# One scheduler, new durations: the order of a gated-scan and two-FFN kernel planned anew

## The chip, the cores and the metric

The kernel runs on one core of one Trainium2 chip, in float32. The metric is the device time of one execution in microseconds (us); lower is better. Shorter durations are given in nanoseconds (ns).

## The reference

Three stages follow each other, for batch 4, 8 heads, 768 steps, head width 48 (so a model width of 384) and a hidden width of 1024.

```python
for t in range(S):                       # 1: gated scan, per head
    state = alpha[t][:, None] * state + outer(k[t], v[t])
    y[t] = q[t] @ state
xk = mu_k*x + (1-mu_k)*x_prev            # 2: first FFN, x_prev is x one step earlier
xr = mu_r*x + (1-mu_r)*x_prev
x  = sigmoid(xr @ w_r) * (relu(xk @ w_k)**2 @ w_v)
h  = relu(x @ w_in)                      # 3: second FFN, 3-tap convolution over time as a gate
out = (h * sigmoid(conv(h, conv_w))) @ w_out
```

## The kernel before

The scan is done by chunks of 128 steps (24 chunks, c = 0 to 23), and the two FFNs by units of 256 steps (12 units, u = 0 to 11; three units make one batch entry). For a chunk, `prep(c)` loads alpha, k, q and v and makes the decays on VectorE: it turns the inputs to lie with the head width on partitions (on TensorE for c < 5, by three 128x512 VectorE transposes after that), runs two VectorE scans over 128x512 elements (`bt`, the suffix products, and `gt`, their counterpart for q), and multiplies k and q with them (`kd`, `qd`). `attend(c)` makes the scores and the state's update, in groups of small matmuls, and `advance(c)` the chunk's output `xt`. In a steady unit the program names, in this order, `stage_k` (x @ w_k and its square, into `bigh` and `bigl`), `stage_r` (the gate), `attend`, `stage_v` (@ w_v, gated, into the pair `xh`, `xl`), `advance` and `prep` two chunks ahead, `stage_h` (@ w_in, the convolution and its gate on VectorE and ScalarE, by eight blocks of 128 hidden columns), the second chunk, the mixes for the next unit, and `stage_o` (@ w_out). Nearly every matmul is made of three: a number is split in a high part and a low part (`xh`, `xl`; `wih`, `wil` and so on), and the product leaves out low times low. Units 0 and 1 are computed while the weights still arrive, with undivided w_r and w_v.

None of this is executed in the order in which it is named. Every call on `pl` (an object of the class `Plan`) only notes an operation with what it depends on and how long it should take. `Plan.cost` gives the duration from the engine, the operation and the elements of a row; `Plan.part` begins a group of matmuls with a fixed extra; `Plan.lag` is the time from one engine's end to another's start, with the transfer time for a DMA. Each operation gets a `tail`, the longest way from its start to the end of the program. `Plan.forward` then plays the program through: on the engine that can begin earliest it takes the operation that is ready, and of several that are ready the one with the longest tail. An operation is not broken off once it has begun. `Plan.backward` computes the tails again from the order found. `Plan.issue` repeats this six times and keeps the order with the earliest modelled end; the instructions are then issued engine by engine in that order, and each engine keeps to it on the chip, waiting where an input is late. Transfers have one queue, SP's, ordered in the same way. Where the plan sees TensorE idle before 30 us, it puts in small matmuls on `ones` ("warm" matmuls), whose results nothing uses.

Which instructions there are is thus the same whatever the durations are, the warm matmuls excepted; their order on each engine, and which buffer each takes, come from the durations. All instructions are recorded at line 303 of the kernel, so that the profile names them by their tiles.

Of the kernel before, what the change touches and what calls it, by code (L numbers as in the profile page):

```python
# [138 lines left out]
class Plan:  # L139
# [58 lines left out]
    def cost(self, eng, fn, args, kw, n):  # L198
        ptr = sum(is_ap(x) and self.size(x) == 1 for x in (*args[1:], *kw.values()))
        ptr = ptr if n > 1 else 0  # L200
        if eng == "vector":
            tensors = sum(is_ap(x) and self.size(x) > 1 for x in (*args[1:], *kw.values()))
            fast = fn in ("tensor_copy", "tensor_scalar") and tensors == 1 and "accum_out" not in kw
            fast = fast and not self.in_psum(args[1])
            return 70 + (0.52 if fast else 1.04) * n + 62 * ptr
        if eng == "scalar":
            return 93 + 0.833 * n + 93 * ptr
        if eng == "gpsimd":
            return 60 + 0.8 * n if fn == "memset" else 150 + (2.1 if fn == "tensor_tensor" else 1.0) * n
        if eng == "sync":  # L210
            return 475.0
        if fn == "transpose":
            return 109.0
        x = args[1].on(args[1].pool.tiles[0]) if isinstance(args[1], Buf) else args[1]
        if x.dtype == F32R:
            return n / 2.2

        rows = 64 if x.shape[0] <= 64 else 128
        width = next(w for w in (32, 64, 128) if self.size(args[1]) <= w)
        return 4 * n / 2.4 * rows / 128 * width / 128 + 3  # L220
# [13 lines left out]
    def part(self):  # L234

        if self.whole:
            self.ops.append(self.whole)
        self.whole = self.op("tensor")
        self.whole.dur += 200.0

    def op(self, eng):
        op = Op()
# [83 lines left out]

    def lag(self, op, s):
        t = self.LAG[op.eng][list(self.LAG).index(s.eng)]
        return t + 650 + op.bytes / 360 if op.bytes else t

    def forward(self, start, spare, until):
        order, free, clock = [], dict.fromkeys(self.LAG, start), Clock()
        dma, flying = start, [0.0] * 8
        todo = {e: [] for e in free}
        for op in self.ops:
            op.left, op.ready = len(op.deps), 0.0
            for r in op.root:
                r.left, r.end, r.tile, r.line.n, r.line.held = len(r.ops), 0.0, None, 0, 0
                r.pool.free = [(0.0, i) for i in range(len(r.pool.tiles))]
            if not op.left:  # L340
                insort(todo[op.eng], (-op.tail, op.i, op))
        for _ in self.ops:
            t, op = self.pick(todo, free)
            e = op.eng
            todo[e].remove((-op.tail, op.i, op))
            dur = op.dur
            if e == "tensor":
                x = free[e]
                idle = min((f for f in spare.free if f[0] < x), default=None) if x < until else None
                while idle and x + 115 * clock.at(x) < t - 50:  # L350
                    x += clock.spend(x, 113.0, 1.0) + 2
                    order.append(spare.tiles[idle[1]])
                    spare.free = [(x + 200, i) if i == idle[1] else (f, i) for f, i in spare.free]
                dur = clock.spend(t, dur, op.share)
            for r in op.root:
                if r.tile is None:
                    r.line.n += 1
                    r.line.held += 1
                    f = min(r.pool.free)
                    r.pool.free.remove(f)  # L360
                    r.slot, r.tile = f[1], r.pool.tiles[f[1]]
            free[e] = op.end = t + dur
            if op.bytes:
                dma = op.end = max(dma, op.end + 650) + op.bytes / 360
                flying = flying[1:] + [dma + 900]
                free[e] = max(free[e], flying[0])
            for s in op.succ:
                s.left -= 1
                s.ready = max(s.ready, op.end + self.LAG[e][list(self.LAG).index(s.eng)])
                if not s.left:  # L370
                    insort(todo[s.eng], (-s.tail, s.i, s))
            for r in op.root:
                r.left -= 1
                r.end = max(r.end, op.end + 150)
                if not r.left:
                    r.line.held -= 1
                    r.pool.free.append((r.end, r.slot))
            order.append(op)
        return order
# [56 lines left out]
def is_ap(x):  # L436
    return isinstance(x, (Buf, bass.AP))
# [704 lines left out]
```

## Time and profile before

| | us |
|---|---|
| time, median of 3 runs | 586.3 (585.58 to 587.22) |
| time of the profiled execution | 584.05 |
| its span, from the first to the last instruction | 582.3 |
| TensorE matmul busy | 559.6 (96%) |
| TensorE weight loads busy | 525.2 (90%) |
| VectorE busy | 492.7 (85%) |
| ScalarE busy | 431.3 (74%) |
| GpSimd busy | 15.8 (3%) |
| mean granted TensorE clock | 0.988 |

The span is what the profiler saw between the first and the last instruction; the execution's own time has 1.75 us around it. In the profile PE is TensorE's matmul stream, PEld its weight loads, DVE is VectorE, ACT is ScalarE, POOL is GpSimd, and SPq the queue that issues transfers. Matmuls are pipelined: one of 256 columns is shown with some 280 ns from start to end, while the next begins much earlier. How fast TensorE really goes is read from the distance between starts.

### The profile page before, as it was taken

What the parts mean: (1) busy time and instruction counts of PE and PEld (TensorE: products, weight loads), DVE (VectorE), ACT (ScalarE), POOL (GpSimd) and SP (SyncE); (2) the same over time, 40 slices, a digit from 0 to 9 for tenths busy, and PEclk for the clock granted to TensorE, in tenths of its full rate; (3) what the DMA queues carried; (4) which work ended last, traced back from release to release, by engine and by line L of the source; (5) the groups of instructions that cost most, each with busy time, mean ns of one, the idle gap of its engine ahead of it and who ended that gap; (6) DMA issues with size and microseconds to landing.
All of it is one profiled execution on the core that took longest, in us unless ns stands there. A gap on an engine that the chain in (4) does not pass through costs nothing.

```text
span 582.3 us, 18585 instructions
## 1 busy us (share of the span) xinstructions
PE 559.6 (96%) x7762; PEld 525.2 (90%) x7762; DVE 492.7 (85%) x1044; ACT 431.3 (74%) x1035; POOL 15.8 (3%) x61
## 2 busy tenths in 40 slices
PE   8679899999989999999999999999999999999997
PEld 7568788999889998998999998998999998999994
DVE  7999999999999889789699789789699789448263
ACT  4799998997668678668668668669659758748563
POOL 3000000000000001000000001000000001000000
PEclk9889999999979999999999999999999999999999
DMA  9998947002432332233132232232132121000000
GB/s 181 213 190 244 247 139 217 16 28 79 113 77 75 73 87 63 56 90 80 40 89 67 54 90 55 66 89 69 51 90 54 41 65 23 22 1 13 18 1 32
DMA packets 87404, 47.99 MB, mean 82 GB/s; under 512 B 49170, under 2 KB 81810, under 8 KB 87314
## 3 DMA queue, kind: packets, MB, share of 16 engines
q1 hardware_dynamic: 87314, 46.74, 32.9%
q8 instruction: 62, 1.02, 0.8%
q14 instruction: 28, 0.23, 0.1%
HBM read 42.00 MB, written 4.72 MB: 80 GB/s over the span
## 4 chain that ended last, share of the span: by engine, by line
PE 60%; DVE 27%; ACT 7%; issue 3%; DMA 1%; POOL 1%; SPq 0%; DVEq 0%; POOLq 0%; ACTq 0%
PE pf L303 52%; DVE tmp L303 7%; PE sc L303 6%; DVE x L303 4%; DVE qd L303 3%; PE kk L303 2%; DVE gt L303 2%; DVE bigl L303 2%; ACT tmp L303 2%; DVE kd L303 2%; ACT raw L303 1%; DVE bt L303 1%; DMA ht<-in_moe_w_v_dram 1%; ACT ht L303 1%; DVE am L303 1%
## 5 line engine op out<-in xcount | busy, mean ns | idle before, releaser
L303 ACT ACTIVATE tmp<-tmp 128x256 f32<-128x256 f32 (+1 forms) x144 | 69.1, 485 | 33.7 <-DVE tt L303 21.6
L303 DVE SCALAR_TENSOR_TENSOR tmp<-ht,cw,tmp 128x256 f32<-128x256 f32 x192 | 86.7, 479 | 5.6 <-ACT tmp L303 4.8
L303 PE MATMUL pf<-bigh,wv 128*128 128x256 f32 x336 | 89.6, 310 | 0.5 <-DVE kd L303 0.3
L303 PE MATMUL pf<-xh,wih 128*128 128x256 f32 x288 | 82.4, 286 | 1.9 <-DVE xl L303 1.0
L303 PE MATMUL pf<-xh,wkh 128*128 128x256 f32 x288 | 79.4, 282 | 3.7 <-ACT xh L303 2.8
L303 PE MATMUL pf<-xl,wih 128*128 128x256 f32 x288 | 81.3, 282 | 1.6 <-DVE xl L303 1.6
L303 PE MATMUL pf<-xl,wkh 128*128 128x256 f32 x288 | 81.3, 284 | 0.6 <-DVE xl L303 0.5
L303 PE MATMUL pf<-xh,wil 128*128 128x256 f32 x288 | 80.9, 281 | 0.0
L303 PE MATMUL pf<-xh,wkl 128*128 128x256 f32 x288 | 80.1, 280 | 0.0
L303 PE MATMUL pf<-bigh,wvh 128*128 128x256 f32 x240 | 68.7, 286 | 1.0 <-DVE bigl L303 0.6
L303 PE MATMUL pf<-bigl,wvh 128*128 128x256 f32 x240 | 67.4, 281 | 0.0
L303 PE MATMUL pf<-woh,bigh 128*128 128x384 f32 x192 | 66.9, 349 | 0.4 <-ACT bigh L303 0.4
L303 PEld LDWEIGHTS pf<-bigh,wv 128*128 128x128 f32 x336 | 63.4, 190 | 3.6 <-ACT x L303 0.6
L303 PE MATMUL pf<-wol,bigh 128*128 128x384 f32 x192 | 65.1, 340 | 0.0
L303 PE MATMUL pf<-woh,bigl 128*128 128x384 f32 x192 | 64.2, 350 | 0.2
L303 ACT ACTIVATE pf<-pf 128x512 f32<-128x512 f32 x88 | 51.1, 584 | 10.9 <-PE pf L303 9.8
L303 PEld LDWEIGHTS pf<-xh,wkh 128*128 128x128 f32 x288 | 54.4, 190 | 4.4 <-ACT xh L303 3.1
L303 PEld LDWEIGHTS pf<-xh,wih 128*128 128x128 f32 x288 | 55.4, 192 | 3.3 <-ACT xh L303 1.3
L303 PEld LDWEIGHTS pf<-xl,wih 128*128 128x128 f32 x288 | 55.3, 192 | 2.1 <-DVE xl L303 2.1
L303 PEld LDWEIGHTS pf<-xl,wkh 128*128 128x128 f32 x288 | 54.8, 190 | 1.6 <-DVE xl L303 1.0
L303 PEld LDWEIGHTS pf<-xh,wil 128*128 128x128 f32 x288 | 55.3, 192 | 0.0
L303 PEld LDWEIGHTS pf<-xh,wkl 128*128 128x128 f32 x288 | 55.0, 191 | 0.0
(164 smaller groups left out, 1391.6 us busy)
## 6 DMA issues: line engine op xcount, KB each, us to landing
vt<-in_v_dram SPq DMA_DIRECT2D x48, 96.0 KB, 3.4
out_dram<-ot SPq DMA_DIRECT2D x23, 192.0 KB, 1.9
sa<-in_alpha_dram SPq DMA_DIRECT2D x38, 96.0 KB, 2.3
sk<-in_k_dram SPq DMA_DIRECT2D x38, 96.0 KB, 2.2
sq<-in_q_dram SPq DMA_DIRECT2D x38, 96.0 KB, 2.3
raw<-in_moe_w_out_dram SPq DMA_DIRECT2D x4, 768.0 KB, 5.3
sk<-in_k_dram SPq DMA_DIRECT2D x38, 80.0 KB, 2.2
sa<-in_alpha_dram SPq DMA_DIRECT2D x38, 80.0 KB, 2.2
```

What stands on the lines that cost most here:

```text
L303: getattr(getattr(self.nc, x.eng), fn)(*args, **kw)
```

## The change

Only the durations of the plan are changed; no operation of the kernel is added, removed or altered.

```diff
@@ def cost(self, eng, fn, args, kw, n):
         ptr = ptr if n > 1 else 0
+        ptr -= kw.get("accum_out") is not None and n > 1
         if eng == "vector":
...
-            return 70 + (0.52 if fast else 1.04) * n + 62 * ptr
+            each = {"tensor_tensor_scan": 2.07, "transpose": 1.7}.get(fn, 0.52 if fast else 1.04)
+            return max(70 + each * n + 62 * ptr, 110)
         if eng == "scalar":
-            return 93 + 0.833 * n + 93 * ptr
+            src = args[1].on(args[1].pool.tiles[0]) if isinstance(args[1], Buf) else args[1]
+            each = 0.81 if self.in_psum(args[1]) else 0.94 if src.ap[-1][0] > 1 else 0.833
+            some = 130 if src.shape[0] == 48 else 0
+            return (65 if each == 0.81 else 93) + each * n + 93 * (ptr + ("accum_out" in kw)) + some
@@ def part(self):
-        self.whole.dur += 200.0
+        self.whole.dur += 250.0
@@ def lag(self, op, s):
-        return t + 650 + op.bytes / 360 if op.bytes else t
+        return t + 650 + op.bytes / 300 if op.bytes else t
@@ def forward(self, start, spare, until):
-                dma = op.end = max(dma, op.end + 650) + op.bytes / 360
+                dma = op.end = max(dma, op.end + 650) + op.bytes / 300
```

In the plan a VectorE scan of 512 elements now takes 1130 ns (602 before), a VectorE transpose of 512 elements 940 ns (602 before), and no VectorE operation less than 110 ns. A ScalarE copy out of PSUM takes 28 ns and 0.023 ns an element less, one that reads every second word 0.107 ns an element more, one on 48 partitions 130 ns more. A group of small matmuls takes 50 ns more, and transfers go at 300 bytes a ns instead of 360.

## Rows read from the trace of the kernel before

**Rows 1.** The page: engine, busy us, share of span, instructions.

```profile
PE 559.6 (96%) x7762; PEld 525.2 (90%) x7762; DVE 492.7 (85%) x1044; ACT 431.3 (74%) x1035; POOL 15.8 (3%) x61
```

**Rows 2.** Windows: stretch, its length, busy us of each engine, clock, DMA share, GB/s.

```profile
core 0: us, PE busy (x) PEld busy (x) DVE busy (x) ACT busy (x) POOL busy (x), PEclk, DMA share, GB/s
0.00:60.00 60.00, 48.84 (x940) 41.73 (x940) 54.03 (x113) 46.67 (x99) 5.95 (x29) 0.94 0.94 207
60.00:105.00 45.00, 41.95 (x413) 37.29 (x414) 44.64 (x79) 41.55 (x87) 0.12 (x1) 1.00 0.66 188
105.00:158.00 53.00, 52.63 (x616) 50.85 (x615) 52.72 (x113) 44.36 (x110) 0.11 (x1) 1.00 0.24 61
159.40:209.30 49.90, 47.03 (x651) 44.76 (x651) 45.87 (x99) 34.03 (x87) 0.11 (x1) 0.93 0.34 82
161.00:169.00 8.00, 6.99 (x33) 6.50 (x34) 7.86 (x15) 3.51 (x10) 0.00 (x0) 0.57 0.53 118
...
209.30:253.80 44.50, 44.30 (x659) 42.05 (x651) 38.41 (x81) 32.11 (x80) 3.17 (x8) 1.00 0.28 68
...
297.40:341.00 43.60, 43.57 (x655) 41.95 (x651) 38.54 (x85) 31.45 (x78) 0.12 (x1) 1.00 0.29 70
```

**Rows 3.** Waits of TensorE from 165 us on: us in total, times, longest.

```profile
PE pf L303 <- DVE bigl L303: 0.6, 1, 0.6
PE pf L303 <- ACT bigh L303: 0.4, 2, 0.2
```

**Rows 4.** TensorE in time: start, us, operation, [idle before <- what ended it].

```profile
157.31 0.28 PE L303 MATMUL pf<-bigh,wvh 128*128 128x256 f32 x1
157.43 0.28 PE L303 MATMUL pf<-bigl,wvh 128*128 128x256 f32 x1
...
159.47 0.38 PE L303 MATMUL pf<-xh,wih 128*128 128x256 f32 x1 [0.38 <-ACT xh L303]
161.00 0.38 PE L303 MATMUL pf<-xl,wih 128*128 128x256 f32 x1 [1.15 <-DVE xl L303]
...
162.42 0.58 PE L303 MATMUL pf<-xh,wih 128*128 128x256 f32 x1 [0.57 <-ACT xh L303]
163.44 0.58 PE L303 MATMUL pf<-xl,wih 128*128 128x256 f32 x1 [0.44 <-DVE xl L303]
163.82 0.42 PE L303 MATMUL pf<-xh,wil 128*128 128x256 f32 x1
164.04 0.42 PE L303 MATMUL pf<-xh,wih 128*128 128x256 f32 x1
```

**Rows 5.** VectorE in time, same columns.

```profile
155.09 1.21 DVE L303 TENSOR_TENSOR_SCAN gt<-ad,rec_f 128x512 f32<-128x512 f32 x1
...
157.07 1.12 DVE L303 STREAM_TRANSPOSE tmp<-sa 128x512 f32<-128x512 f32 x1
158.01 0.77 DVE L303 TENSOR_TENSOR pf<-pf,x 128x512 f32<-128x512 f32 x1
...
159.13 1.23 DVE L303 TENSOR_TENSOR_SCAN bt<-ad,one_l 128x512 f32<-128x512 f32 x1
160.28 0.67 DVE L303 TENSOR_TENSOR xl<-pf,xh 128x512 fp32r<-128x512 f32 x1
...
161.85 1.22 DVE L303 TENSOR_TENSOR_SCAN gt<-ad,rec_f 128x512 f32<-128x512 f32 x1
162.99 0.40 DVE L303 TENSOR_TENSOR xl<-pf,xh 128x256 fp32r<-128x256 f32 x1
```

**Rows 6.** TensorE in time: the next scores after these.

```profile
199.37 0.69 PE L303 MATMUL sc<-qd,kd 48*64 48x64 f32 x32
```

**Rows 7.** Chain that ended last: start, us until the next piece, what.

```profile
46.77 6.15 DMA ht<-in_moe_w_v_dram
...
134.54 1.02 DVE kd L303
...
155.17 1.13 DVE gt L303
```

**Rows 8.** VectorE by form: operation xcount | busy us, mean ns | idle before.

```profile
L303 DVE STREAM_TRANSPOSE kd<-sk 128x512 f32<-128x512 f32 x19 | 21.0, 1106 | 0.0
```

## The prediction

> **What bounds the kernel now.** I read the page first. TensorE's matmuls are busy for 559.6 of 582.3 us, VectorE's instructions for 492.7 [rows 1]. That is a mean over parts with different limits, so I cut the span into windows where the pattern of the page changes [rows 2].
>
> From 0 to 105 us VectorE is the fullest engine: 54.03 of 60 us and then 44.64 of 45. The transfers are busy too, 0.94 of the first 60 us. Here the weights are brought in, narrowed and split, and TensorE fills in. From 105 to 158 us both engines are full: TensorE 52.63 and VectorE 52.72 of 53. From 209 us on TensorE alone is: one unit takes 44.5 or 43.6 us, TensorE is busy for 44.30 or 43.57 of them, and VectorE for about 38.5.
>
> Is a busy TensorE also a fast one? In the list of its instructions in time, matmuls of 256 columns begin 0.12 us apart where nothing disturbs them [rows 4], though each is shown as 0.28 long. From 165 us to the end the view of waits has 1.0 us in all for TensorE [rows 3]. An order alone can therefore win next to nothing behind 165 us.
>
> The one place that stands out lies between. The first `stage_h` matmul of unit 2 begins at 159.47, and to the same point of unit 3 it is 49.90 us, against 43.60 for the unit at the same place of its batch entry, 297.4 to 341.0 [rows 2]. That is 6.3 us too long. The rows of TensorE say why: at the start of `stage_h` it waits 0.38 us for `xh`, 1.15 for `xl`, 0.57 for `xh` and 0.44 for `xl` [rows 4], 2.5 us in all. [...]
>
> What is VectorE doing then? It is never idle there, so this is a question of order. The product `pf<-pf,x` and the two splits `xl` are what TensorE waits for. Ahead of the product stand a `gt` scan and a transpose of alpha, ahead of the first split a `bt` scan, ahead of the second another `gt` scan, each 1.1 to 1.2 us [rows 5]. The transpose and the last two scans belong to `prep(8)`, the ninth of the 24, whose `qd` is first read by the scores at 199.37 [rows 6], some 35 us later. (The chain names a transfer in this stretch, but VectorE's rows run without a gap, so it was not what held the split.)
>
> **The change part by part.** No instruction is removed or added but warm matmuls, so every cost here is that of an order.
>
> The plan's view of VectorE. Per `prep` from chunk 5 on, two scans go from 602 to 1130 ns and three transposes from 602 to 940: 2 x 0.528 + 3 x 0.338 = 2.07 us. Are the new numbers right? In the chain, where a piece lasts until the next instruction can begin, a scan takes 1.13 us and a transpose 1.02 [rows 7]; so the plan was wrong by about that much, and the new one is close. `prep(6)` and `prep(7)` run between 134 and 157 us, in the stretch in which VectorE has no idle time to make good: the old plan has VectorE 2 x 2.07 = 4.1 us earlier there than it is. An order made for that clock sees an idle VectorE and slips in `prep(8)`; on the chip the gap isn't there and the scans delay the product and the splits. With the new durations the same greedy rule finds them ready together at that point and takes the one with the longer tail, which is the product or the split.
>
> [...]
>
> Term A, unit 2. At most the 6.3 us go, at least nothing. I take what the rows price: waits 2.5 us, and the low clock, which follows a stall. At a mean of 0.57, 0.43 / 0.5 x 8 = 6.9 us are at the lower level, of which TensorE works from about 163.8 to 168.5 (an estimate); 4.7 us at half speed lose 2.4. A = 2.5 + 2.4 = **4.9 us**. The work that is put off, the rest of `prep(8)`, must find room: from 209 us on VectorE idles 44.5 - 38.41 = 6.1 us a unit.
>
> Term B, 0 to 105 us. Six preps run here; scans, ScalarE copies and transfers all have other durations, so this order changes as a whole. VectorE is idle for 5.97 + 0.36 = 6.3 us of it [rows 2], some of it before the first data; that bounds the gain. On the other side one more exposed weight transfer costs 6.15 us, as that of `w_v` at 46.77 does [rows 7]. The plan's 300 bytes a ns is still above the 207 GB/s that were moved in the first 60 us, so on the transfers it stays optimistic. I take **0** and keep -6.3 and +6.2.
>
> Term C, from 165 us on. Gain at most the 1.0 us of waits [rows 3]. A loss is possible if preps are put where they hold up `stage_h` (second rival). I take **0**, since TensorE's other work hides VectorE's there now.
>
> The rest: ScalarE's new copy times, some tens of ns each, the 50 ns on a group and the floor of 110 ns change nothing on the chip but through the order, and ScalarE has slack (44.36 of 53 us at its fullest late stretch). Warm matmuls lie in TensorE's idle time at the start, where VectorE and transfers bind; more or fewer cost nothing there. I cost them at 0.
>
> Sum against the profiled execution: 584.05 - 4.9 = 579.2 us. The median of the runs shown is 2.25 us above that execution, so 581.4 us is what I expect of a median.
>
> **The rivals.** First: the stall is traded for another. VectorE is full from 60 to 165 us, so what is not done early must be done later, and the product can be freed only to let the next thing wait, a `kd` for the scores or the mix for unit 3. For it: 52.72 of 53 us. Against it: `prep(8)` has some 35 us to spare. Time: as before, 586.3. [...]
>
> Second, slower: preps planned longer are moved into `stage_h`. In the seven units from 165 to 473 us, VectorE's convolution steps are a chain of their own, and one more transpose (1.02 us) between them that TensorE's other work doesn't cover makes `bigh` late for `stage_o`. Seven times 1.02 are 7.1, less 4.9: 588.5 us; with a scan as well, up to 596. It decides from 4.9 / 7 = 0.7 us a unit. For it: units differ only by where preps stand, and the plan must put 2.07 us more a prep somewhere. Against it: the 1.0 us of waits now, with such instructions already in these places.
>
> Third: the start gets worse by exposed weight transfers, because SP's queue is in a new order too and a load that waits for its buffer holds all behind it. One such transfer leaves 581.4 + 6.15 = 587.5, two give 593.7. For it: transfers are busy 0.94 of the first 60 us; against it: only one of them is in the chain for that long.
>
> **How the numbers follow.** Within 0.3% (1.8 us) is about what a measurement of this kernel can't tell from no change. Forecast, 0.57: its own range is 575 (A whole, and more from the start) to 584.5. First rival, 0.13, and the third with one transfer, 0.06, are within 0.3%. Second rival, 0.18, and the third with two, 0.06, are slower. So faster 0.57, same 0.19, slower 0.24. For the range I leave out two exposed transfers (0.06), the upper part of the second rival (0.07) and a gain of over 11 us (0.06): 575.0 to 590.5 us.
>
> **What would show it.** If A is right, `pf<-pf,x` and `xl` of unit 2 stand ahead of the scans on VectorE, the four waits at the start of its `stage_h` are gone or under 0.5 us each, the clock stays at 1.0 around there, and that unit takes 44 to 45 us instead of 49.9. If B is right, TensorE is full from about 105 us on as before. If C is right, later units stay at 43.6 to 44.5 us. The prediction is wrong if the stretch up to the first full unit moves by more than a few us in either direction: then term B, which I can't price but by bounds, was the larger one. Units of over 45 us would mean the second rival.

## The result, and the profile after

The median went from 586.46 us (585.58 to 587.22, 4 runs) to 570.7 us (570.11 to 571.62, 4 runs): a ratio of 0.9733 [0.9713, 0.9753], 2.7% faster. That is below the range of the prediction. The profiled execution took 570.11 us. Its span is 14.0 us shorter than that of before, and the medians differ by 15.8 us, because the profiled execution of before, which is not one of the four, lay 2.4 us below their median and that of after 0.6 below its own.

The span first, then the engines of the page of after, which answer to [rows 1], and the clock in 40 slices:

```profile
span 568.3 us, 18585 instructions
PE 551.7 (97%) x7778; PEld 522.4 (92%) x7778; DVE 490.8 (86%) x1044; ACT 429.8 (76%) x1035; POOL 15.6 (3%) x61
PEclk9789999999999999999999999999999999999999
```

TensorE's 16 more instructions are warm matmuls (96 instead of 80). The windows of after, cut at the same events as those of [rows 2]:

```profile
core 0: us, PE busy (x) PEld busy (x) DVE busy (x) ACT busy (x) POOL busy (x), PEclk, DMA share, GB/s
0.00:60.00 60.00, 50.89 (x952) 43.70 (x956) 56.52 (x114) 48.50 (x99) 5.98 (x29) 0.91 0.94 209
60.00:105.00 45.00, 43.86 (x498) 39.44 (x488) 43.04 (x82) 40.41 (x89) 0.12 (x1) 1.00 0.62 177
105.00:157.00 52.00, 50.29 (x606) 47.72 (x604) 52.00 (x110) 44.09 (x108) 0.11 (x1) 1.00 0.24 62
157.00:165.00 8.00, 8.00 (x78) 7.97 (x71) 7.46 (x18) 7.01 (x21) 0.00 (x0) 1.00 0.51 117
157.00:200.20 43.20, 43.20 (x660) 41.91 (x652) 42.43 (x93) 31.25 (x81) 0.12 (x1) 1.00 0.35 88
200.20:244.00 43.80, 43.80 (x655) 42.49 (x651) 41.97 (x91) 34.38 (x86) 2.51 (x8) 1.00 0.31 78
286.80:329.90 43.10, 43.10 (x659) 41.82 (x651) 38.65 (x85) 31.25 (x78) 0.33 (x1) 1.00 0.28 72
```

Unit 2 (157.0 to 200.2) takes 43.2 us instead of 49.9, and its first 8 us have a granted clock of 1.00, where 161 to 169 us had 0.57 before. VectorE shows why. In [rows 5] a transpose of `prep(8)` stood ahead of the product, and a scan of `prep(8)` ahead of each of the two splits; after:

```profile
151.96 1.23 DVE L308 TENSOR_TENSOR_SCAN bt<-ad,one_l 128x512 f32<-128x512 f32 x1
153.10 0.67 DVE L308 TENSOR_TENSOR pf<-pf,x 128x512 f32<-128x512 f32 x1
...
154.35 1.22 DVE L308 TENSOR_TENSOR_SCAN gt<-ad,rec_f 128x512 f32<-128x512 f32 x1
155.48 0.66 DVE L308 TENSOR_TENSOR xl<-pf,xh 128x512 fp32r<-128x512 f32 x1
...
157.07 0.41 DVE L308 TENSOR_TENSOR xl<-pf,xh 128x256 fp32r<-128x256 f32 x1
157.40 0.34 DVE L308 TENSOR_TENSOR ss<-ss,tt 128x192 f32<-128x192 f32 x1
157.67 1.08 DVE L308 STREAM_TRANSPOSE tmp<-sa 128x512 f32<-128x512 f32 x1
```

These two scans are the last of `prep(7)`; the first transpose of `prep(8)` now starts at 157.67, behind the last split. TensorE has no wait left at the place of [rows 4]:

```profile
157.03 0.38 PE L308 MATMUL pf<-xh,wih 128*128 128x256 f32 x1
157.25 0.28 PE L308 MATMUL pf<-xl,wih 128*128 128x256 f32 x1
157.36 0.29 PE L308 MATMUL pf<-xh,wil 128*128 128x256 f32 x1
```

For the whole program I cut the span at the first `stage_h` matmul of units 2, 3 and 10, from the list of TensorE's instructions (us). The experiments below are cut at the same events, and each row is one profiled execution:

| kernel | start | unit 2 | units 3 to 9 | rest | span |
|---|---|---|---|---|---|
| before | 159.5 | 49.9 | 308.2 | 64.7 | 582.3 |
| after | 157.0 | 43.2 | 303.4 | 64.7 | 568.3 |
| e1, VectorE's durations | 164.1 | 43.1 | 302.5 | 64.7 | 574.4 |
| e2, all but VectorE's | 161.0 | 49.1 | 308.0 | 64.6 | 582.7 |
| e3, new until unit 2 | 157.6 | 43.6 | 308.5 | 64.7 | 574.4 |
| e4, new from unit 3 | 161.2 | 49.8 | 303.5 | 64.6 | 579.1 |
| e5, `prep(8)` held back | 162.0 | 46.5 | 310.3 | 64.5 | 583.3 |
| e6, short scans, old order | 158.7 | 44.2 | 303.7 | 64.6 | 571.2 |
| e7, VectorE and ScalarE | 162.1 | 43.6 | 303.8 | 64.7 | 574.2 |
| e8, VectorE and transfers | 157.9 | 44.0 | 304.1 | 64.5 | 570.5 |
| e9, scans only | 166.3 | 44.9 | 305.7 | 64.6 | 581.5 |
| e10, transposes only | 157.6 | 45.6 | 304.4 | 65.8 | 573.4 |
| e11, transfers at 330 | 166.9 | 43.1 | 303.5 | 64.6 | 578.1 |
| e12, transfers at 270 | 164.8 | 43.6 | 304.0 | 64.6 | 577.0 |
| e13, 270, no warm matmuls | 162.4 | 43.6 | 303.6 | 64.6 | 574.2 |
| e14, 330, no warm matmuls | 158.5 | 43.1 | 303.5 | 64.7 | 569.8 |
| e15, changed, no warm matmuls | 159.3 | 43.1 | 303.4 | 64.6 | 570.4 |

The 14.0 us are 2.5 of the start, 6.7 of unit 2 and 4.8 of units 3 to 9. Within the start 3.6 us are won up to the first `stage_h` matmul of all (93.1 us instead of 96.7), and 1.1 are lost between there and unit 2: TensorE is busy for 50.29 of 52.00 us from 105 us on, where it was for 52.63 of 53. Units 3 to 9 are the surprise. In the view of waits TensorE's 1.0 us behind 165 us [rows 3] has become 0.5, so it explains 0.5 of the 4.8:

```profile
PE pf L308 <- ACT bigh L308: 0.5, 1, 0.5
```

Where the rest was lost shows in the distance between starts. In units 3 to 9 the time from each matmul on `woh` or `wol` to the next matmul sums to 66.6 us before and to 63.5 after: 3.1 of the 4.8 us are in `stage_o` (0.9 are in the small matmuls, 0.5 in `stage_k`). Unit 4 before, first TensorE, then VectorE:

```profile
272.50 0.34 PE L303 MATMUL pf<-woh,bigh 128*128 128x384 f32 x1
272.68 0.33 PE L303 MATMUL pf<-wol,bigh 128*128 128x384 f32 x1
273.13 0.44 PE L303 MATMUL pf<-woh,bigl 128*128 128x384 f32 x1
273.41 0.33 PE L303 MATMUL pf<-woh,bigh 128*128 128x384 f32 x1
```

```profile
268.93 1.11 DVE L303 STREAM_TRANSPOSE kd<-sk 128x512 f32<-128x512 f32 x1
269.88 1.08 DVE L303 STREAM_TRANSPOSE qd<-sq 128x512 f32<-128x512 f32 x1
270.82 0.40 DVE L303 TENSOR_TENSOR tmp<-tmp,ht 128x256 f32<-128x256 f32 x1
...
272.63 0.44 DVE L303 TENSOR_TENSOR bigl<-tmp,bigh 128x256 fp32r<-128x256 f32 x1
```

Undisturbed, these matmuls start 0.17 to 0.18 us apart. The one on `bigl` starts 0.45 us after its forerunner and 0.06 after the split of `bigl` ends (272.63 + 0.44), with two transposes of a `prep` ahead of that split in VectorE's row, which has no idle time from there to the split. About 0.28 us are lost, and yet no wait is printed and the rows overlap or nearly touch, because a matmul is shown as 0.33 long. The same stage of unit 4 after:

```profile
262.37 0.34 PE L308 MATMUL pf<-woh,bigh 128*128 128x384 f32 x1
262.54 0.34 PE L308 MATMUL pf<-woh,bigl 128*128 128x384 f32 x1
262.71 0.34 PE L308 MATMUL pf<-woh,bigh 128*128 128x384 f32 x1
```

### The profile page after: what moved, and what is told of

Its sections match the earlier page's. It is cut to its first block, busy times and chain, and to the rows that moved or that the text cites. A ratio compares the mean times of both kernels' runs of the same rounds, so it can differ in the third digit from the quotient of the medians.

```text
span 568.3 us, 18585 instructions
## 1 busy us (share of the span) xinstructions
PE 551.7 (97%) x7778; PEld 522.4 (92%) x7778; DVE 490.8 (86%) x1044; ACT 429.8 (76%) x1035; POOL 15.6 (3%) x61
## 4 chain that ended last, share of the span: by engine, by line
PE 76%; ACT 9%; DVE 6%; DMA 2%; issue 0%; POOL 0%; SPq 0%; ACTq 0%; DVEq 0%; POOLq 0%
PE pf L308 66%; PE sc L308 7%; DVE tmp L308 3%; PE kk L308 3%; ACT raw L308 2%; ACT x L308 1%; DMA raw<-in_moe_w_out_dram 1%; ACT tmp L308 1%; ACT bigh L308 1%; DVE x L308 1%; DMA vt<-in_v_dram 1%; DVE qd L308 1%; ACT pf L308 1%; ACT ub L308 1%; ACT ht L308 0%
## 5 line engine op out<-in xcount | busy, mean ns | idle before, releaser
L308 DVE SCALAR_TENSOR_TENSOR tmp<-ht,cw,tmp 128x256 f32<-128x256 f32 x192 | 84.8, 477 | 5.6 <-ACT tmp L308 5.4
L308 PE MATMUL pf<-xh,wih 128*128 128x256 f32 x288 | 80.6, 281 | 1.1 <-DVE xl L308 1.1
L308 PE MATMUL pf<-xl,wih 128*128 128x256 f32 x288 | 79.7, 277 | 0.0
L308 PE MATMUL pf<-xh,wil 128*128 128x256 f32 x288 | 79.7, 277 | 0.0
L308 PE MATMUL pf<-woh,bigl 128*128 128x384 f32 x192 | 62.7, 342 | 0.4 <-DVE bigl L308 0.4
L308 PEld LDWEIGHTS pf<-xh,wih 128*128 128x128 f32 x288 | 54.1, 188 | 2.2 <-DVE xl L308 1.4
L308 PEld LDWEIGHTS pf<-xl,wih 128*128 128x128 f32 x288 | 54.1, 188 | 0.0
L308 PEld LDWEIGHTS pf<-xh,wil 128*128 128x128 f32 x288 | 54.1, 188 | 0.0
```

Source lines behind the costliest of these rows:

```text
L308: getattr(getattr(self.nc, x.eng), fn)(*args, **kw)
```

## The experiments

The theory after the result: VectorE's durations alone make the gain, in unit 2 by `prep(8)` and in units 3 to 9 by splits that come less late; the start is another matter. The rivals: the other durations made it, or the start's new order did and carries on. Ratios are against the kernel before on the same chip.

**One half of the durations each.** e1 sets only VectorE's, e2 only the rest (ScalarE, group, transfers).

```diff
+            each = {"tensor_tensor_scan": 2.07, "transpose": 1.7}.get(fn, each)     # e1 alone
+            return max(70 + each * n + 62 * ptr, 110)                               # e1 alone
```

> The plan gets only VectorE's new durations (scan 2.07 ns an element, transpose 1.7, floor 110 ns); ScalarE, groups and transfers keep the old ones. Theory (the gain comes from VectorE's scans and transposes, which were planned 2.07 us a prep too short): nearly all of it, 569 to 574 us against 586.5 before, with the unit of the stall (unit 2) at 43 to 44.5 us instead of 49.8 and stage_o of the later units 0.4 to 0.8 us shorter each. Rival (the other durations, ScalarE's above all, made it): under half of the gain, 579 us or more. Second rival (no duration as such: any new order drawn from this planner scatters by so much): anything, with no likeness to the changed kernel in unit 2 or in the later units.

> The complement: ScalarE's, the groups' and the transfers' new durations, VectorE's old ones. Theory: no more than a fifth of the gain, 583 to 588 us, with the stall at the start of stage_h of unit 2 still there and later units at 43.6 to 44.5 us. Rival (the other durations made it): 578 us or less. Second rival (scatter): it moves by 5 us or more in either direction.

e1: 576.71 us, over the 569 to 574 expected, 0.9871 [0.985, 0.9893]. e2: 583.86 us, 0.9982 [0.997, 0.9994]. Unit 2 and units 3 to 9 are mended by e1 (43.1 and 302.5) and not by e2 (49.1 and 308.0). e2 does shorten `stage_o` (64.3 us of units 3 to 9, worked out as above), but its small matmuls take 43.2 instead of 40.8. The start of e1, 164.1, is 7 us later than that of the changed kernel, and so the two halves don't add up to the whole. That is where e1 missed.

**One stretch of the program each.** A flag switches all new durations: on until unit 3 is planned (e3), or from there on (e4).

```diff
             c0 = 2 * u + 2
+            if u == 3:
+                pl.new = False        # e3; e4 starts with False and sets True here
```

> All new durations for the operations that the program names up to unit 2 (with prep 8 and 9), the old ones for all of units 3 to 11. Theory (three separate gains: 2.4 us before stage_h of unit 2, 6.7 us in unit 2, 4.9 us in the units behind it): the first two come and the third does not, 9 us less than before, about 577 us, and units 3 to 9 stay as long as before. Rival (the later units are faster only because VectorE enters them with less work left over from the start): all of the gain, 571 us.

> The reverse: the old durations for what is named up to unit 2, the new ones for units 3 to 11. Theory: only the third gain, 5 us less than before, about 581.5 us, with the stall in unit 2 as before and stage_o of units 3 to 9 shorter by 0.4 to 0.8 us each. Rival (the later gain is the start's): 586 us.

e3: 577.01 us, 0.9876 [0.9858, 0.9894]; e4: 579.63 us, 0.9913 [0.9897, 0.993]. e3 has the short unit 2 (43.6) and the old units 3 to 9 (308.5); e4 the reverse (49.8 and 303.5). The two gains don't depend on each other, and what happens in units 3 to 9 is not carried over from the start.

**The stall of unit 2 alone.** All durations are old; VectorE's part of `prep(8)` must wait for the last split.

```diff
             x = stage_v(big, g)
+            last_split = pl.ops[-1]
...
+                    n0 = len(pl.ops)
                     prep(c0 + 2)
+                    if u == 2:
+                        for op in pl.ops[n0:]:
+                            if op.eng == "vector":
+                                op.deps.add(last_split)
```

> All the old durations; the plan is only told that no VectorE operation of prep 8 may begin before the last split of unit 2's stage_v. Theory (the stall at the start of unit 2's stage_h is prep 8 standing ahead of the product and the splits): unit 2 goes from 49.9 to 43.2 to 45 us with the clock at 1.0 there, the start and the later units stay within 0.5 us of before, so 5 to 6.5 us less than before. Rival (VectorE is full and the product must wait for one thing or another): unit 2 stays over 48 us, or the units 3 and 4 get as much longer.

582.44 us, 0.996 [0.9944, 0.9975], 2.4 us less than before where 5 to 6.5 were expected; the profiled execution was the slowest, with 585.1. Its units 2 and 3:

```profile
162.00:208.50 46.50, 44.45 (x660) 41.80 (x652) 45.58 (x99) 33.84 (x85) 0.12 (x1) 1.00 0.35 90
208.50:254.60 46.10, 45.31 (x652) 42.21 (x652) 39.70 (x84) 32.35 (x82) 3.18 (x8) 1.00 0.28 73
```

The clock is at 1.00 (0.93 in unit 2 before [rows 2]), so the low clock did follow the stall, and unit 2 is 3.4 us shorter. But it is not 43, and unit 3 takes 46.1 us instead of 44.5. By the distances between starts `stage_h` of unit 2 is mended wholly (8.3 us, as after the change, where it was 13.9), and its small matmuls and its `stage_o` take 1.2 us more each: what was put off came back late. That the plan's short scans are the reason is an inference. The first rival of the prediction has that much right.

**The scans' own time in the old order.** From `prep(6)` on both scans run over 32 elements instead of 512; costs and order of the plan are those of before.

```diff
+            if c >= 6:                # after each of the two scans of prep
+                op = pl.ops[-1]
+                (fn, args, kw), = op.parts
+                op.parts = [(fn, [x if isinstance(x, float) else x[:, 0:32] for x in args], kw)]
```

> The old durations and exactly the old order; only the two VectorE scans of the preps 6 to 23 run over 32 elements instead of 512 (the output is no longer the reference's). It takes about 1 us of VectorE time a scan away without a change of order. Theory (from unit 3 on, VectorE's preps hold up the blocks that stage_o reads, in waits too short to be shown): units 3 to 9 fall to about 43.0 us with stage_o at 11.2 to 11.6, and the stall of unit 2 shrinks by 3 us or more: 575 to 580 us. Rival (the later units are slower in the old order for a reason on TensorE itself, such as how its small groups are mixed in): units 3 to 9 stay at 43.6 to 44.5 us and only unit 2 shrinks, 581 to 583 us.

573.03 us, even less than the 575 to 580 expected, 0.9803 [0.9779, 0.9827]. Units 3 to 5:

```profile
202.90:246.60 43.70, 43.51 (x659) 41.86 (x651) 34.80 (x81) 32.35 (x80) 3.18 (x8) 1.00 0.28 70
246.60:289.80 43.20, 43.20 (x623) 41.90 (x611) 33.67 (x77) 32.54 (x80) 0.10 (x1) 1.00 0.28 71
289.80:332.90 43.10, 43.10 (x661) 41.85 (x651) 35.07 (x85) 31.31 (x78) 0.12 (x1) 1.00 0.28 71
```

With nothing moved, VectorE's shorter scans give 5.7 us in unit 2 and 4.5 in units 3 to 9, of which 3.6 in `stage_o` (66.6 to 63.0). So VectorE's time lay on the path in units in which it is idle for 6 us and TensorE shows hardly a wait. That answers where term C failed.

**Which of VectorE's durations.** e9 corrects the scans alone, e10 the transposes alone, both without the floor of 110 ns.

```diff
+            each = {"tensor_tensor_scan": 2.07}.get(fn, each)      # e9
+            each = {"transpose": 1.7}.get(fn, each)                # e10
```

> Only the scan's duration is new (1130 instead of 602 ns), transposes keep 602. Theory (any large part of VectorE's missing time in the plan mends unit 2 and the later units; scans are 1.06 of 2.07 us a prep): unit 2 at 44 to 47 us, units 3 to 9 at half of the way, 43.3 to 44.2. Rival (the scans are what matters, transposes were right): as with both, units 3 to 9 at 42.8 to 43.9. The start is not forecast.

> Only the transpose's duration is new (940 instead of 602 ns), scans keep 602. Theory: as with the scans alone, about half of the way in unit 2 and in the later units. [...]

e9: 583.22 us (579.95 to 584.0), 0.9961 [0.994, 0.9983]; e10: 575.21 us, 0.9849 [0.981, 0.9888]. In unit 2 the scans give 5.0 us and the transposes 4.3, in units 3 to 9 they give 2.5 and 3.8: either takes part of the plan's error away, and e1, with both, gives 6.8 and 5.7. The transposes were thus priced wrongly as well: 602 ns for 512 elements in the old plan, a mean of 1106 ns in the trace of before [rows 8]. e9's late start (166.3) takes most of its gain back.

**The start.** e7 and e8 add ScalarE's durations or the transfers' rate to e1; e11 and e12 are the whole change with 330 and 270 bytes a ns instead of 300, in `lag` (shown) and in `forward`.

```diff
-        return t + 650 + op.bytes / 300 if op.bytes else t
+        return t + 650 + op.bytes / 330 if op.bytes else t          # e11; e12: 270
```

> VectorE's and ScalarE's new durations, groups and transfers the old ones. With VectorE's alone the start was 7 us longer up to stage_h of unit 2 than with all (164.1 against 157.0). Theory (the start is shared by VectorE and ScalarE, and a plan that corrects only one of them puts the other's work late): the start comes to 156 to 159, the whole to 571 us. Rival (the transfers' rate made the start): the start stays over 161, the whole at 575 us or more. Second rival (the order of the start is a matter of chance): any value, also above 164.

> VectorE's durations and the transfers' rate new, ScalarE's and the groups' old. Theory: the start stays over 161, the whole at 575 us or more, unit 2 and the later units as with VectorE's durations alone. Rival (the transfers' rate made the start): the start at 156 to 159, the whole at 571 us.

> The whole change, but transfers planned at 330 bytes a ns instead of 300. Theory (a lower rate in the plan makes the start better, because it is nearer to what transfers do): the start up to stage_h of unit 2 lies between the 157.0 of the changed kernel and the 162.1 seen at 360 with VectorE's and ScalarE's durations, the later units as in the changed kernel: 571 to 576 us. Rival (the start is drawn by chance with every new order): it scatters over 155 to 165 with no regard to the rate.

> The whole change, but transfers planned at 270 bytes a ns. Theory: the start at 157 or earlier, 568 to 571 us. Rival (chance): scatter over 155 to 165 with no regard to the rate, so it may well lie at 160 or later here.

e7: 575.33 us, 0.9836 [0.9814, 0.9857]; e8: 572.15 us, 0.9787 [0.975, 0.9824]; e11: 577.59 us, 0.9869 [0.9841, 0.9896]; e12: 579.25 us, 0.9895 [0.9853, 0.9937]. In all four, unit 2 (43.1 to 44.0) and units 3 to 9 (303.5 to 304.1) are as in the changed kernel; only the start differs. By e7 ScalarE's durations don't make it (162.1, where 156 to 159 was expected). By e8 I took the lower rate for the cause; e11 (166.9 at 330) fits that and e12 (164.8 at 270) doesn't, so this theory fell as well. The start does not follow the rate: 157.0 at 300, 8 to 10 us later on either side of it.

One thing that is different in them is the number of warm matmuls: 212 in e11 and 262 in e12, 96 in the changed kernel. The group in e11 from 0 to 45 us, and the two longest waits in it:

```profile
L1111 PE MATMUL pf<-ones 128*64 128x64 f32 x212 | 18.2, 244 | 5.5 <-issue 4.5 <-DVE ones L1018 1.1
```

```profile
22.89 0.68 PE L1111 MATMUL pf<-ones 128*64 128x64 f32 x9 [2.79 <-issue]
33.58 0.62 PE L1111 MATMUL pf<-ones 128*64 128x64 f32 x7 [1.67 <-issue]
```

In 4.5 us TensorE waits at a warm matmul for nothing that the profile shows; in the changed kernel the same group has no such wait:

```profile
L1107 PE MATMUL pf<-ones 128*64 128x64 f32 x96 | 9.1, 261 | 1.1 <-DVE ones L1014 1.1
```

So three runs leave the warm matmuls out, with the order otherwise kept: e13 from e12, e14 from e11, e15 from the changed kernel.

```diff
-        warm = lambda x: nc.tensor.matmul(x[0:64, 0:64], ones, ones, start=True, stop=True)
+        warm = lambda x: None
```

> The order planned at 270 bytes a ns, instruction for instruction, without its 262 warm matmuls. Theory (the draws of the start with 98 to 262 warm matmuls are slow because TensorE, which keeps to the order, runs them while real work is ready, and because its next instructions come late, which the waits name issue, 1.7 to 4.5 us): the issue waits go and stage_h of unit 2 starts at 157 to 161 instead of 164.8, 571 to 575 us. Rival (the order on the other engines and the transfers' queue made the start late): 163 or later, 577 us or more. Second rival (without the warm matmuls the clock stays low in the start and takes it all back): later than 164.8.

> The order planned at 330 bytes a ns without its 212 warm matmuls. Theory: stage_h of unit 2 starts at 158 to 162 instead of 166.9, 571 to 575 us. Rival (other engines' order): 165 or later, 577 us or more.

> The changed kernel's own order without its 96 warm matmuls, for which it shows no issue wait. Theory: they lie in idle time here, so that the start stays within 1.5 us of 157.0 and the whole at 569 to 572 us. Rival (the warm matmuls hold the clock up and the start needs it): 2 us or more slower.

e13: 576.12 us, 0.9839 [0.9805, 0.9873]; e14: 572.75 us, 0.978 [0.9749, 0.981]; e15: 571.62 us, 0.9754 [0.9724, 0.9783]. In the profiled executions the start comes 8.4 us earlier in e14, 2.4 earlier in e13 and 2.3 later in e15. But each is one execution, and one order spreads too: up to 152 us e4 and e5 have the order of before on every engine, and yet the same scan of `prep(7)` starts up to 3 us apart in before, e4 and e5:

```profile
150.95 1.23 DVE L303 TENSOR_TENSOR_SCAN bt<-ad,one_l 128x512 f32<-128x512 f32 x1
152.70 1.22 DVE L313 TENSOR_TENSOR_SCAN bt<-ad,one_l 128x512 f32<-128x512 f32 x1
154.00 1.23 DVE L306 TENSOR_TENSOR_SCAN bt<-ad,one_l 128x512 f32<-128x512 f32 x1
```

So the 2.4 of e13 and the 2.3 of e15 (within 1.5 was expected) show nothing by themselves, and the intervals of e13 and e12, and of e15 and the change, overlap. Only e14 is clear of it: its interval lies below that of e11. A part of its 8.4 us is the draw as well, since e11's profiled execution was its slowest (579.94) and e14's its fastest (571.6). By the two ratios, 0.9869 and 0.978, the 212 fillers cost about 5 us. How TensorE's first 40 us change from e11 to e14:

```profile
0.00:40.00 40.00, 34.47 (x650) 30.12 (x651) 33.07 (x66) 22.76 (x46) 4.55 (x23) 0.96 0.99 194
```

```profile
0.00:40.00 40.00, 29.72 (x515) 24.45 (x516) 36.19 (x77) 28.66 (x58) 4.56 (x23) 0.87 1.07 204
```

Without the 212 fillers TensorE is less busy and at a lower clock (0.87 against 0.96), and VectorE and ScalarE get further in the same time (77 and 58 instructions instead of 66 and 46). So the fillers of e11, put where the plan saw TensorE idle, stood in the way of real work. The rest of the spread stays open. e13's 162.4 fits neither what the theory expected nor its rival. Fillers don't explain e1 and e8 either: e1 has 86, none of them with such a wait, and starts unit 2 at 164.1; e8 has 134 and starts it at 157.9. e1 loses 3.0 of its 7 us behind the first `stage_h` matmul of all, where the fillers are long over, and TensorE has one long wait there:

```profile
PE pf L306 <- ACT ht L306: 2.7, 1, 2.7
```

## Why the prediction was wrong

- **Term A, unit 2: right mechanism, too small.** Product and splits stand ahead of the scans of `prep(8)`, the four waits are gone, the clock is 1.00. It gave 6.7 us where 4.9 were summed, and where the bound from the trace was 6.3: the unit that served as measure was itself slowed by what term C overlooked (the same unit takes 43.1 us after, not 43.6). The rows' price left out 1.8 us. The half speed in its 2.4 us is measured: before, the granted clock is 0.50 from 162.0 to 168.5 us, where undelayed matmuls of 256 columns begin 0.21 us apart (0.12 from 168.84 us on). By the distances between starts 5.6 of the 6.7 us are in `stage_h` and 0.7 in the small matmuls, which the sum had at nothing. The waits were read too small in the way of term C: the matmul at 161.00 starts 1.53 us after that at 159.47, where 0.12 is undisturbed, so 1.4 us were lost and 1.15 printed; and the first of the four, 0.38, ends where the unit begins and is no part of it. e6 gets 5.7 us there by shorter scans without any new order.
- **Term C, units 3 to 9: the step that failed.** It was "An order alone can therefore win next to nothing behind 165 us", with a bound of 1.0 us from the view of waits [rows 3]. It gave 4.8; that TensorE's other work hides VectorE's there did not hold. A TensorE busy for 44.30 of 44.5 us [rows 2] was not one that lost nothing: busy counts overlapping matmuls (in unit 4 one is shown as 0.34 us long and the next begins 0.18 later), and a late input stretched the distance between two starts there from 0.18 to 0.45 us with no gap printed. The 6 us a unit in which VectorE is idle were read as slack for the same reason; its work was late at single places, not short of time. e4 gives 4.7 of it alone, e3 nothing, and e6 shows by the unmoved order that VectorE's late scans cost it.
- **Term B, the start: taken as 0, -2.5 in the profiled executions, inside its bounds.** The plan's orders of the start, with all of VectorE's durations right and the warm matmuls kept, range from 157.0 to 166.9 us (e1, e7, e8, e11, e12 and the change). The change has the earliest, which is luck. So 11.5 us (A and C) come from truer durations of VectorE, and the rest is a draw that went well. How large that rest is stays open: 2.5 us lie within the 3 us by which one order spreads, and the medians, 15.8 us apart, leave an estimated 4.3; a rate of 330 instead of 300 would have left a ratio of 0.9869 instead of 0.9733.
- **"Warm matmuls ... I cost them at 0": not shown wrong for this change, wrong for the order of e11.** The 96 of the change make no difference clear of noise (e15), but the 212 of e11 cost about 5 us (e14).
- **The rivals.** A stall traded for another happens when only the place is mended (e5: unit 3 takes 46.1 us instead of 44.5), not when the plan is. Nor did the time stay as before: 11.5 us came from VectorE's order, 4.8 of them in units 3 to 9. The second, preps moved into `stage_h`, made no unit slower: units 3 to 9 take 42.8 to 43.8 us after, 43.6 to 44.5 before. The third, a start made worse, is what e1, e7, e11 and e12 drew (162.1 to 166.9 us) and the change did not.
- **The sum.** Of 9.1 us of span that the forecast missed, 4.8 are term C, 2.5 the start and 1.8 the size of A. No kernel of the experiments was faster than the changed one; the intervals of e15, e8 and e14 overlap its own.

## What to carry to other kernels

A planner that orders by estimated durations is worth feeding with measured ones, for the engine whose estimates are furthest off first; here two operations, both planned at little over half their time on the chip (602 ns, against 1130 for a scan and 1020 for a transpose to the next start [rows 7]), made 11.5 of the 14.0 us. Before a wait view is taken for a bound, compare the distances between starts of one kind of matmul with their undisturbed distance, since that is where the 0.28 us of unit 4 showed for which no wait was printed. The start of this kernel, in which the weights are brought in, narrowed and split, came out up to 10 us apart from order to order and 3 us apart for one and the same: cut such a start off from the rest when two orders are compared, try several, and don't read a few us of it from one profile each.

## What the runs showed that was not expected

Inputs that came late cost TensorE 4.8 us over seven units while its idle time shows only 0.5 us less. Matmuls whose results nothing uses delayed real work in e11: with 212 of them in the first 45 us TensorE had 4.5 us of waits without a cause in the profile, and the program took about 5 us longer than without them, though the granted clock of the first 40 us was higher. And one and the same order of instructions spread by 3 us over the first 150 us from one profiled execution to another.
